# Thirty-five extra transposes of v in seven attention steps of a DMA-bound kernel

## The chip, the cores and the metric

The kernel runs on one core of one Trainium2 chip. The metric is the device time of one execution in microseconds, and a comparison is a difference of means over several executions.

In the lines of the profile PE is TensorE's matmuls and PEld its weight loads, DVE is VectorE, ACT is ScalarE, POOL is GpSimd and SP is SyncE; a q behind such a name is the engine's issuing of DMAs. A *fetch* is one DMA packet with a block of TensorE's own program (the row q8 instruction of a page: 41 packets, all of 16384 bytes, in the kernel before). A store has *landed* when all 16 of its completion packets have been written.

Three sources of numbers appear below, and they are kept apart. *Times* are of unprofiled executions and of the one profiled run. *Spans* are from the first to the last instruction in the profile; a span is usually about 1.7 us shorter than the time. *Trace positions* are times within the profiled run, counted from the start of its span.

## The reference, cut to what matters

Attention with a forgetting decay over 8 batches, 8 heads, 576 rows and head size 64; its result goes through a spectral mix with 64 modes, whose weights are two 64 x 512 x 512 float32 arrays.

```python
cum = np.cumsum(np.log(np.clip(f, 1e-4, 1.0)), axis=-1)
scores = scale * q @ k.T + cum[:, :, :, None] - cum[:, :, None, :]   # causal
attn = softmax(scores) @ v                     # (8, 8, 576, 64)
x = attn.transpose(0, 2, 1, 3).reshape(8, 576, 512)
X = rfft(x, axis=1)                            # modes 0..63 are mixed
Yr = Xr @ w_r - Xi @ w_i                       # per mode, 512 x 512
Yi = Xr @ w_i + Xi @ w_r
u = x + irfft(Y, n=576)
out = u + np.maximum(u @ w_ch, 0.0)            # (8, 576, 512) f32
```

The mode weights are 64 x 512 x 512 x 2 x 4 bytes = 134 MB as float32 in memory. They are streamed once through a ring of nine tiles, and they are what the kernel waits for: from 287.9 to 400.2 us their transfers make up 110.9 of the 112.3 us of the chain of waits in the trace of the kernel before.

## The kernel before

Attention runs in 32 steps, one head of a pair of batches at a time. Each step transposes five blocks of v back into rows. This is the place that the change touches:

```python
NRING = 9
STG = 3
...
def emit_vback(s):
    dc, bp, h = steps[s]
    c0 = 2 * bp * H + 2 * dc + h
    vp = psT.tile([128, NSB, 2, Dh], BF16, tag="tr", name="vp")
    for sc in range(NSB):                       # NSB = 5 blocks
        nc.tensor.transpose(
            vp[:, sc, :, :].rearrange("p b d -> p (b d)"),
            VTs[s // 2 % 2][:, h, sc * 128 : (sc + 1) * 128],
            ident_bf[:, :],
        )
    va = vap.tile([128, NSB, 2, Dh + 1], BF16, tag="va", name="va")
    nc.vector.tensor_copy(va[:, :, :, 0:Dh], vp[:, :, :, :])
    ...
```

The weights are loaded ahead into the ring and used tile by tile; a load is issued when its slot comes free:

```python
wpool = ctx.enter_context(tc.tile_pool(name="wpool", bufs=NRING))
...
def emit_w_load(n):                             # on GpSimd's DMA queue
    ...
    for t, src in enumerate((moe_w_r, moe_w_i)):
        pool_dma(wb[t:128:2, :, :], src[...])
...
def emit_modes(n, fill=None):                   # the matmuls on tile n, into A
    ...
    if n == NT - 1:                             # the last tile
        for mi in range(nm):
            ...                                 # matmuls on the weights
            fill(mi, hf)                        # matmuls of the first output job
            add_y(mi, mi + 1)
```

After the last tile come the output jobs. For each, TensorE makes `pu` and `pz` in PSUM, ScalarE copies `pu`, VectorE joins both, and SyncE issues the stores:

```python
def emit_u(job, ps, u, split=False):
    ...
    nc.scalar.copy(u[:, bs, :], ps[0][:, bs, :])

def emit_o(job, ps, u, o, pair, split=False):
    ...
    nc.vector.scalar_tensor_tensor(
        o[:, bs, :], ps[1][:, bs, :], 0.0, u[:, bs, :], ALU.max, ALU.add)
    ...
    nc.sync.dma_start(out[...], o[...])         # 27 stores in all
...
for n, job in enumerate(jobs):
    last = n == len(jobs) - 1
    zs = terms(job, ps, 1, "xy" if n else "y")
    ...
    run(zs, us)
    ...
    emit_u(jobs[n + 1], nxt, uo_n[0])
    emit_o(job, ps, *uo, n == 0)
```

The softmax here doesn't subtract the row's maximum and nothing guards it: scores larger than these inputs give would overflow.

## Time and profile before

The time was 436.51 us, the median of 3 runs (436.29 to 437.32).

| point in the trace of before | us |
|---|---|
| attention's last transposes of v begin | 268.9 |
| last weights landed | 400.2 |
| VectorE's last output instruction ends | 427.1 |
| span ends | 435.2 |

The rows of the page that matter, and the chain of waits, are shown in the prediction. (It counts the page's 40 slices from 0; this text counts them from 1.)

### The profile page before, as it was taken

To read this page: it belongs to the slowest core of one execution; us is meant where nothing else is said; L and a number is where in the kernel's file an instruction comes from. 1 tells how busy PE (TensorE), PEld (TensorE's weight loads), DVE (VectorE), ACT (ScalarE), POOL (GpSimd) and SP (SyncE) were. 2 spreads that over 40 slices of the span, in tenths; PEclk is the share of its full clock that TensorE was granted. 3 is DMA by queue.
4 is the path that set the end of the run, shared out by engine and by line. 5 is a ranking of instruction groups with operands and counts; after the bars stand their busy time and mean duration, and the time that the engine had idled before them with its cause. 6 is when DMAs were issued, how large, how long until landed. Compare 5 with 4: busy or idle time off the path is not lost.

```text
span 435.2 us, 12314 instructions
## 1 busy us (share of the span) xinstructions
PE 368.1 (85%) x5313; PEld 249.7 (57%) x5313; DVE 263.7 (61%) x659; ACT 224.4 (52%) x339; POOL 126.8 (29%) x198
## 2 busy tenths in 40 slices
PE   3787799999987879778787788799999998899881
PEld 2454566776666666566565666656665555454540
DVE  5797888876555655555557568533332665553892
ACT  2887488774526454365462646134434443631781
POOL 8333332333233233232333222223223223200400
PEclk9996899996558665586565869589999999989997
DMA  8999999999999999999999999999999999995797
GB/s 184 234 235 241 234 236 238 235 212 236 234 215 236 225 224 237 210 238 233 214 237 211 212 211 212 211 211 211 211 211 211 212 210 211 211 211 100 253 367 274
DMA packets 50982, 97.38 MB, mean 224 GB/s; under 512 B 3792, under 2 KB 12976, under 8 KB 50928
## 3 DMA queue, kind: packets, MB, share of 16 engines
q0 software_dynamic: 46560, 86.09, 100.9%
q1 hardware_dynamic: 4368, 10.51, 6.7%
q8 instruction: 41, 0.67, 0.6%
q14 instruction: 13, 0.11, 0.1%
HBM read 163.73 MB, written 9.44 MB: 398 GB/s over the span
## 4 chain that ended last, share of the span: by engine, by line
PE 35%; DMA 26%; ACT 12%; DVE 10%; issue 4%; SPq 0%; DVEq 0%; POOL 0%; ACTq 0%
DMA wb<-in_moe_w_i_dram 25%; ACT E L576 8%; PE pav L614 7%; PE ps L569 7%; PE A L188 6%; PE tp L307 5%; PE px L657 2%; PE vp L541 2%; DVE QTs L322 2%; ACT KT L320 2%; ACT VT L326 2%; DVE XT L671 1%; DVE os L1005 1%; DVE E L591 1%; PE px L682 1%
## 5 line engine op out<-in xcount | busy, mean ns | idle before, releaser
L576 ACT ACTIVATE E<-ps 128x1024 bf16<-128x1024 f32 (+1 forms) x128 | 101.5, 851 | 26.1 <-PE ps L569 15.4
L93 POOL DMA_DIRECT2D wb<-in_moe_w_r_dram x64 | 42.5, 664 | 128.9 <-PE A L188 25.1
L188 PE MATMUL A<-XT,wb 128*128 128x16 bf16 x1984 | 69.9, 181 | 8.2 <-DMA wb<-in_moe_w_i_dram 3.8
L188 PEld LDWEIGHTS <-wb 128*128 128x128 bf16 x1984 | 63.5, 100 | 22.8 <-issue 11.9
L569 PE MATMUL ps<-QTs,KT 64*128 64x64 bf16 (+4 forms) x384 | 60.2, 334 | 16.6 <-ACT E L576 14.7
L93 POOL DMA_DIRECT2D wb<-in_moe_w_i_dram x64 | 42.3, 661 | 77.5 <-DMA wb<-in_moe_w_i_dram 32.5
L614 PE MATMUL pav<-va,E 128*128 128x65 bf16 (+1 forms) x1088 | 57.1, 214 | 3.2 <-DVE x_all L636 2.6
L614 PEld LDWEIGHTS <-E 128*128 128x128 bf16 (+1 forms) x1088 | 47.0, 118 | 16.9 <-issue 7.0
L591 DVE TENSOR_TENSOR E<-E,trimask 128x256 bf16<-128x256 bf16 (+2 forms) x128 | 36.9, 303 | 20.0 <-ACT E L576 19.8
L326 ACT COPY VT<-tp 128x640 bf16<-128x640 bf16 (+1 forms) x32 | 23.2, 761 | 33.4 <-PE tp L307 33.4
L867 ACT CAST XW<-pxw 128x512 bf16<-128x512 f32 x36 | 20.7, 586 | 35.9 <-PE pxw L860 28.3
L569 PEld LDWEIGHTS <-KT 64*128 64x128 bf16 x384 | 19.4, 100 | 33.6 <-issue 22.8
L860 PE MATMUL pxw<-wch,yy 128*128 128x512 bf16 x144 | 36.0, 388 | 0.0
L320 ACT COPY KT<-tp 128x640 bf16<-128x640 bf16 (+1 forms) x32 | 21.9, 749 | 26.0 <-PE tp L307 25.8
L910 ACT CAST XW<-pB 128x512 bf16<-128x512 f32 x36 | 21.0, 585 | 25.4 <-PE pB L828 25.3
L909 DVE CAST x_all<-pA 128x512 bf16<-128x512 f32 x36 | 24.9, 692 | 14.2 <-PE pA L828 12.5
L322 DVE COPY QTs<-tp 128x640 bf16<-128x640 bf16 (+1 forms) x32 | 23.4, 767 | 14.3 <-PE tp L307 14.0
L636 DVE TENSOR_TENSOR x_all<-pav,rcp 128x384 bf16<-128x384 f32 x64 | 29.1, 455 | 0.9
L625 DVE RECIPROCAL rcp<-pav 128x6 f32<-128x6 f32 x64 | 12.1, 189 | 25.1 <-PE pav L614 24.3
L828 PEld LDWEIGHTS <-ident_bf 64*64 64x64 bf16 (+1 forms) x348 | 15.7, 108 | 17.9 <-issue 9.3
L153 DVE TENSOR_TENSOR YTe<-A,Yacc 128x128 bf16<-128x128 f32 x16 | 5.9, 367 | 33.3 <-PE A L188 33.3
L541 PE MATMUL vp<-ident_bf,VT 128*128 128x128 bf16 x160 | 18.4, 261 | 4.6 <-DVE QTs L322 3.9
(142 smaller groups left out, 617.4 us busy)
## 6 DMA issues: line engine op xcount, KB each, us to landing
wb<-in_moe_w_r_dram POOLq DMA_DIRECT2D x62, 512.0 KB, 16.7
wb<-in_moe_w_i_dram POOLq DMA_DIRECT2D x62, 512.0 KB, 17.3
stv<-in_v_dram POOLq DMA_DIRECT2D x10, 576.0 KB, 15.2
out_dram<-os SPq DMA_DIRECT2D x10, 512.0 KB, 4.5
stk<-in_k_dram POOLq DMA_DIRECT2D x11, 288.0 KB, 15.3
stq<-in_q_dram POOLq DMA_DIRECT2D x11, 288.0 KB, 15.1
wx<-in_v_dram POOLq DMA_DIRECT2D x5, 576.0 KB, 15.4
out_dram<-uo SPq DMA_DIRECT2D x3, 512.0 KB, 3.6
```

What stands on the lines that cost most here:

```text
L93: keep(nc.gpsimd.dma_start(dst, src))
L188: ins = nc.tensor.matmul(A[:, eb, mi, :], lhsT=w_of(mi, eb * 128), rhs=x_of(m), start=(i == 0), stop=(i == len(terms) - 1),)
L320: nc.scalar.copy(rows(KTs[pr % 2][:, :, 0:S]), tv)
L322: ins = nc.vector.tensor_copy(rows(QT[pr][:, :, :]), tv)
L326: nc.scalar.copy(rows(VTs[pr % 2][:, :, 0:S]), tv)
L541: nc.tensor.transpose(vp[:, sc, :, :].rearrange("p b d -> p (b d)"), VTs[s // 2 % 2][:, h, sc * 128 : (sc + 1) * 128], ident_bf[:, :],)
L569: nc.tensor.matmul(ps[:, b, o : o + n], lhsT=KTs[pr % 2][bs, h, jb * 128 : (jb + 1) * 128], rhs=QT[pr][bs, h, jb * 128 + c0 : jb * 128 + c ...
L576: nc.scalar.activation(E[:, :, piece * 512 : piece * 512 + w], ps[:, :, 0:w], ACT.Exp, scale=scale,)
L591: nc.vector.tensor_tensor(dg, dg, tr, ALU.mult)
L614: nc.tensor.matmul(pav[64 * half : 64 * half + w, slot, :], lhsT=E[:, b, c : c + (w - 1) * st + 1 : st], rhs=va[:, jb, b, :], start=(n == ...
L636: nc.vector.tensor_tensor(xo, pi, ri, ALU.mult)
L860: nc.tensor.matmul(pxw[:, :], lhsT=xT[:, eb, i * 128 : (i + 1) * 128], rhs=wch[:, eb, :], start=(eb == 0), stop=(eb == NDC - 1),)
```

## The change

The change puts 35 more TensorE transposes into steps 16 to 22, five per step. They rewrite block 0 of v at the same place in PSUM with the same values, so nothing is computed differently. The intent is not the work but its 70 TensorE instructions (a weight load and a matmul each): TensorE's program is fetched in blocks of 16384 bytes (in the kernel before one fetch for every 254 recorded instructions in the mean), and 70 instructions more ahead of the tail let the block borders, and so the fetches, fall at other places among the last tiles and stores.

```diff
     NRING = 9
     STG = 3
+    VREP = range(16, 23)
...
-            for sc in range(NSB):
+            for sc in [0] * (5 if s in VREP else 0) + list(range(NSB)):
                 nc.tensor.transpose(
                     vp[:, sc, :, :].rearrange("p b d -> p (b d)"),
```

## The prediction

> **What bounds the kernel now.** I read the page's head and DMA rows first, then the chain of waits from 394 us to the end, then busy times by stage, then the DMA view of short windows, because the change claims to act on when instruction fetches happen.
>
> The page of the kernel before:
>
> ```profile
> span 435.2 us, 12314 instructions
> DMA  8999999999999999999999999999999999995797
> GB/s 184 234 235 241 234 236 238 235 212 236 234 215 236 225 224 237 210 238 233 214 237 211 212 211 212 211 211 211 211 211 211 212 210 211 211 211 100 253 367 274
> q8 instruction: 41, 0.67, 0.6%
> ```
>
> The 16 DMA engines are busy from the first slice to about 396 us: the weights stream at 211 to 240 GB/s without a hole. There is one hole of about 10 us (slice 36, 100 GB/s), and then the output stores. The q8 row is the fetch of TensorE's own program: 0.67 MB in 41 packets is 16384 bytes each, and the packet records of the trace confirm that size for all 41.
>
> The chain that ended last, from 394 us on, and the last issues:
>
> ```profile
> 384.77 15.42 DMA wb<-in_moe_w_i_dram
> 400.23 0.36 PE A L172 x8
> 401.31 0.86 PE plw L813 x4
> ...
> 421.62 1.24 DVE os L1005
> ...
> 425.46 0.63 PE pz L828 x4
> ```
>
> ```profile
> 426.46 0.68 DVE L1005 SCALAR_TENSOR_TENSOR uo<-pz,uo 128x512 f32<-128x512 f32 x1
> 428.25 2.49 SPq L1012 DMA_DIRECT2D out_dram<-uo  x2
> ```
>
> So there are three stages that set the end: the weights' last landing at 400.2 us; a tail of TensorE, ACT and DVE that makes output tiles (DVE ends at 427.1 us); and the stores, which end 6 us after DVE. In the packet records the last store's packets are written at 433.06 us. From 417 us on, the store queue is never empty, and each 512 KB store lands 1.22 to 1.26 us after the one before it (422.79, 424.01, 425.26, 426.49 us): the stores' end is bound by DMA bandwidth, and by the slowest of the 16 engines, because a store has landed only when all of them have.
>
> Busy times by stage (columns: stretch, its length, then busy time and count of PE, PEld, DVE, ACT, POOL, granted clock, DMA share, GB/s):
>
> ```profile
> 141.00:160.00 19.00, 15.89 (x240) 11.77 (x238) 11.31 (x31) 9.17 (x14) 5.84 (x9) 0.68 1.13 226
> 160.00:180.00 20.00, 16.43 (x209) 12.02 (x206) 10.34 (x30) 10.11 (x14) 6.27 (x10) 0.50 1.13 225
> 180.00:205.00 25.00, 20.91 (x306) 15.64 (x306) 15.37 (x40) 11.94 (x16) 7.04 (x12) 0.67 1.13 227
> 287.00:322.00 35.00, 35.00 (x515) 22.44 (x514) 11.46 (x31) 14.05 (x25) 11.70 (x17) 1.00 1.12 211
> 355.00:370.00 15.00, 13.07 (x204) 7.79 (x204) 8.50 (x17) 6.34 (x11) 5.00 (x7) 1.00 1.12 211
> 370.00:385.00 15.00, 13.02 (x144) 6.88 (x140) 7.86 (x16) 8.16 (x15) 3.28 (x6) 0.89 1.12 211
> ```
>
> In the steps that change (143 to 204 us) TensorE is busy 83% at a clock of 0.5 to 0.7. From 287 to 355 us it is busy all the time and works off a backlog. From 355 us on it idles again, because it waits for weights.
>
> [...]fetches come every 8 to 12 us, on average every 254 recorded TensorE instructions. [...] The packet records give the hold: 0.88 to 1.02 us beside weights, but 1.27 us at 405.21 us and 1.46 us at 416.25 us, among stores:
>
> ```profile
> q1 hardware_dynamic: 207, 0.77, 97.4%
> q8 instruction: 1, 0.02, 4.5%
> ```
>
> (the DMA view of 416 to 418 us.) [...] The trace shows 0.5 and 1.0 in turn up to 285 us, then 1.0.
>
> **The change part by part.** Nothing is removed. Each of steps 16 to 22 transposes block 0 of v six times instead of once, into the same PSUM place; the result is the same.
>
> First, TensorE work. 35 transposes are 35 weight loads and 35 matmuls, 70 instructions. The five transposes of a step start 94 to 100 ns apart in steps 16, 18, 19, 20, 21, 22 and 55 ns apart in step 17 (full clock). Sum: 5 x (95 + 55 + 96 + 100 + 94 + 100 + 94) ns = 3.2 us. The built programs show that the scheduler also moves some neighbours in those steps, and that the last 5,717 of TensorE's instructions are the same in both; GpSimd's and SyncE's order does not change.
>
> Second, whether that reaches the weights. The queue of weights is deep: a 512 KB transfer lands 13 to 20 us after its issue, though one takes 2.4 us at 211 GB/s. The shallowest place is the issue at 279.80 us, which lands at 292.6 us; the transfer ahead of it ends at 288.3 us. Issued 3.2 us later, at 283.0 us, it still has 5 us of queue ahead. So the DMA has no hole and the last weights land at 400.2 us as before.
>
> Third, whether TensorE is in time for them. From each tile's landing and its first matmul, TensorE's lag is 34.5 us at 277 us, 7.9 us at 322 us, 0.9 us at 355 us, and from then on it is 0.7 us or less: it waits for weights. It idles 41.0 - 36.3 = 4.7 us between 355 and 396 us. A backlog larger by at most 3.2 us is gone before the last tile. Cost on the path: 0.
>
> Fourth, the fetches. In the tail each block border comes 70 instructions sooner. Counting back 70 TensorE instructions from where they are now: 396.93 goes to about 395.5 us, 405.21 to about 401.1 us, 416.25 to about 413.6 us. And a border that lay just past the end (10433 + 254 = 10687 of 10665 recorded) now lies inside: old place 10617, about 423.4 us. So 42 fetches instead of 41, if a fetch is made that near the end.
>
> What each is worth: 396.93 to 395.5 stays on an engine that is busy with weights, same hold: 0. 405.21 to 401.1 moves from the first stores into the hole, where DMA does nothing; but the store queue runs dry once more at 412 us, so what it cost was already given back: 0 to -0.2. 416.25 to 413.6: now it hits the first packets of a new batch. The completion packets of the store issued at 415.17 us are written by 15 engines at 417.3 to 417.4 us and by the last about 1.9 us later; the lag of this one engine is 1.0 us at 422 us and about 0.45 us at 428 us [...], and at the end the last engine ends at 433.06 us where most end by 432.4 us. Moved to 413.6 us, it has the dips at 415.7 and 419.4 us to catch up: worth up to -0.7 us. The new fetch at 423.4 us has only the dip at 425.6 us, worth about 0.5 us by the same engine's record: it starts 1.3 to 1.5 us late and ends 0.8 to 1.0 us late, so +0.8 to +1.0. Sum: about +0.1 to +0.3 us if the 42nd fetch is made (I give this 0.75), about -0.7 us if not. Expected: about 0; I add 0.1 us for the risk of the backlog: 436.6 us.
>
> **The rivals.** (a) The added transposes reach the end: the backlog of TensorE is not worked off, since some idle time after 355 us belongs to waits on ACT and DVE rather than on weights. Against it: 4.7 us of idle time for 3.2 us. It would give 437.5 to 439. (b) The fetches cost more than their ring time: a fetch on the engine that carries the last weights (396.93 us now) sets the landing at 400.2 us, or the one at 405.21 us holds up the moves of yl that the first output tiles need. Then the move to 401.1 us, or a changed overlap, gains about 1 us: 435.3 to 435.8. For it: at 405 us moves that landed 1.7 us after issue begin to take 3.2 us. Against it: the tiles that need those moves come some 6 us later. (c) The clock: [...] It would show as a higher granted clock from 143 to 205 us, and still give nothing, since the DMA queue sets the weights' end.
>
> **Range and chances.** Everything that can move is of the size of one fetch, 0.5 to 1.5 us, on 436.5 us; three runs of the kernel before spread over 1.0 us. So 435.6 to 437.7 us should hold it 8 times in 10. 2% is 8.7 us; nothing here comes near: faster 0.01, within 2% 0.98, slower 0.01.
>
> **What would show each step.** Transposes: vp has 195 matmuls instead of 160, DMA keeps 211 GB/s to 396 us, and the chain's last weights land within 0.5 us of 400.2 us. Backlog: TensorE's idle time from 355 to 396 us falls from 4.7 to 1.5 to 3 us. Fetches: q8 counts 42; in the tail they stand near 395.5, 401, 413.6 and 423.4 us. End: the completion packets of the stores after 424 us have one straggler, and between 416 and 422 us hardly any. I am wrong if the last weights land later than 401 us, if the count stays 41 and the time falls by 0.6 us or more, or if the stores' end moves by more than 1 us with DVE's end in place.

The sum came to "about +0.1 to +0.3 us" if the 42nd fetch is made, and its terms (0 to -0.2, up to -0.7, +0.8 to +1.0) are estimates from the trace of the kernel before. The "0.5 and 1.0 in turn" are the granted TensorE clock. The hole and the dips that it names are these in the same trace: the DMA share was 0.00 and 0.02 in the two microseconds from 401 to 403 us, 0.78 from 412 to 413 us, 0.86 from 415 to 416 us, 0.76 from 419 to 420 us and 0.90 from 425 to 426 us, and 0.94 to 1.08 in the other microseconds from 408 to 431 us.

## More of the kernel before

One more row is needed later, the granted TensorE clock in tenths:

```profile
PEclk9996899996558665586565869589999999989997
```

Each of its 40 digits is about 10.9 us of the span. From the tenth slice to the twenty-seventh (about 98 to 294 us) the clock is mostly below full and often near half; after that it is nearly always full.

## The result, and the profile after

The changed kernel took 437.19 us, the median of 6 runs (436.66 to 437.87), against 436.40 us (436.16 to 437.32) for 6 runs of the kernel before in the same rounds. The ratio is 1.0017, with a 95% interval of 1.0004 to 1.003: the mean time of one kernel's runs over that of the other's of the same rounds, so not quite the ratio of the two medians. It is within 2%, and about 0.7 us slower. All outputs are right. The profiled run of the changed kernel was its fastest (436.66 us), so its span of 434.9 us must not be read as a gain over 435.2 us.

First the page of the changed kernel:

```profile
span 434.9 us, 12366 instructions
PEclk9996899998767957759557778699999999999997
GB/s 188 232 235 241 234 236 239 235 212 236 233 216 236 224 225 237 212 237 232 216 237 212 211 212 211 211 211 212 211 211 211 211 211 211 211 211 105 245 389 260
q8 instruction: 42, 0.69, 0.6%
```

The GB/s row is the old one to within a few digits: the weights stream as before. There is one fetch more. The clock row is higher than before in many of the slices from the tenth on. That begins ahead of the change, whose first step lies at 143 us in the fourteenth slice, and so it must not be put down to the change without more.

The instructions on the tile vp, kernel before and then kernel after (count, then minimum, median and maximum in ns, first and last start):

```profile
L541 PE MATMUL vp<-ident_bf,VT x160: 216/230/315, 22.4 to 268.9; 128*128 128x128 bf16 x160
```

```profile
L542 PE MATMUL vp<-ident_bf,VT x195: 216/222/314, 22.4 to 264.7; 128*128 128x128 bf16 x195
```

The 35 transposes are there, and the last transpose of the kernel starts 4.2 us *earlier*, not later. Busy times by stage show how (kernel after; the columns are those in the prediction):

```profile
141.00:160.00 19.00, 15.80 (x257) 12.14 (x254) 11.89 (x32) 9.19 (x14) 5.96 (x9) 0.77 1.13 226
160.00:180.00 20.00, 16.41 (x243) 12.79 (x238) 10.77 (x32) 10.26 (x14) 6.52 (x10) 0.69 1.13 225
180.00:205.00 25.00, 19.34 (x350) 14.95 (x348) 14.88 (x44) 14.53 (x19) 6.85 (x12) 0.80 1.13 227
```

The granted clock rose from 0.68, 0.50 and 0.67 to 0.77, 0.69 and 0.80. TensorE does more matmuls in less busy time. Is it the change that does this? In one pair of traces it looks so, but the 14 traces of the whole study are more careful witnesses:

| | granted clock, 98 to 141 us | granted clock, 143 to 204 us | attention's last transpose of v begins, us | TensorE idle, 355 to 396 us |
|---|---|---|---|---|
| repeats in steps 16 to 22 (after, `a2`, `s256`, `s256b`) | 0.73, 0.78, 0.75, 0.73 | 0.75, 0.75, 0.75, 0.70 | 263.8 to 265.8 | 5.1 to 6.5 |
| no repeats there (10 traces, the kernel before among them) | 0.62 to 0.82, mean 0.69 | 0.61 to 0.72, mean 0.66 | 263.3 to 269.5 | 3.3 to 6.7 |

From 143 us on the clock is higher with the repeats, though the best of the ten others (0.72) passes the lowest of the four. But the same four traces had a clock above the others' mean already from 98 to 141 us, before any repeat. So it is not shown that the repeats raise the clock. When attention ends, and how long TensorE idles later, overlaps fully. Two traces of one and the same program (`end36` and `end36b`, below) begin that last transpose at 269.5 and at 264.0 us, so the 4.2 us between before and after are within what unchanged code does. Neither moved the end, because the weights set it: the last of them landed at 399.33 to 400.67 us in all 14 traces. The idle time of TensorE ahead of the last weights, in the kernel before and then after, is what is left of these stretches:

```profile
355.00:396.00 41.00, 36.33 (x514) 20.96 (x512) 22.22 (x41) 19.12 (x33) 8.58 (x13) 0.96 1.09 205
```

```profile
355.00:396.00 41.00, 34.66 (x494) 20.01 (x495) 22.02 (x41) 18.57 (x32) 8.60 (x13) 1.00 1.09 206
```

41.00 - 36.33 = 4.7 us became 41.00 - 34.66 = 6.3 us. The chain that ended last, kernel after, from its last weights on (start in us, us, what):

```profile
384.31 15.42 DMA wb<-in_moe_w_i_dram
399.74 0.05 issue
399.78 0.36 PE A L173 x8
...
423.75 1.22 DVE os L1006
...
425.01 0.63 PE pz L829 x4
```

The last weights landed at 399.74 us instead of 400.2 us, and all that follows in TensorE and VectorE keeps that distance (VectorE's last output instruction ends at 426.69 us instead of 427.14 us). What differs is the DMA engines' work. The DMA view of 416 to 418 us, where the kernel before had a fetch (shown in the prediction), has in the kernel after only stores (packets, MB, and the time of the packets as a share of 16 engines):

```profile
q1 hardware_dynamic: 227, 0.81, 101.8%
```

and the DMA view of 425 to 427 us, kernel before and then after:

```profile
q1 hardware_dynamic: 271, 0.65, 96.1%
```

```profile
q1 hardware_dynamic: 269, 0.75, 97.6%
q8 instruction: 1, 0.02, 2.9%
```

The fetch of 416.25 us has moved ahead of those stores, and a new one stands among the final ones. In the packet records the fetches from 396 us on are these, with the time that each held its engine:

| | before | predicted after | after |
|---|---|---|---|
| among the last weights | 396.93 (0.88 us) | 395.5 | 396.73 (0.88 us) |
| before or in the first stores | 405.21 (1.27 us) | 401.1 | 401.61 (1.35 us) |
| in the later stores | 416.25 (1.46 us) | 413.6 | 413.96 (0.94 us) |
| new, the 42nd | none | 423.4 | 425.48 (0.92 us) |

### A ruler for the tail

Single runs of either kernel spread over about 1 us or more, so one needs a measure with less noise. From the end of the last matmul on weights (called *the last A*) to VectorE's end is 26.45 to 26.68 us in all 14 traces, whether before, after or an experiment. What comes before the last A is the arrival of weights and the clock, and it moved by 1.4 us between traces (399.98 to 401.38 us). What comes after VectorE's end is stores and fetches. So I compare the time from the last A to the landing of the last store, and call it *the tail*.

The numbers in the next table come from the records of the stores' landings and of the fetch packets. All times are counted from the last A; stores are numbered 0 to 26.

| | tail | fetches, at | store 10 | store 11 | store 17 | store 20 | store 26, the last |
|---|---|---|---|---|---|---|---|
| before | 32.79 | 4.6, 15.7 | 15.8 | 19.1 | 24.7 | 26.6 | 32.8 |
| after | 32.99 | 1.5, 13.8, 25.3 | 17.5 | 18.7 | 24.3 | 27.5 | 33.0 |

Before, the fetch at 15.7 us shows as a jump of 3.3 us between stores 10 and 11. After, that fetch comes earlier (13.8 us), and store 17 is 0.4 us ahead. Then the new fetch shows as a jump of 1.6 us between stores 19 (25.9) and 20 (27.5), and the lead is lost. How far the last of a store's 16 completion packets is behind the median one tells the same: before, 1.97 us at store 11 and still 0.69 us at store 26, 13.7 us later; after, 1.67 us at store 20 and still 1.22 us at store 26, 5.5 us later. So 1.28 us were made up behind the one fetch, and 0.45 us behind the later one. There is one pair of traces here; the experiments give more. (The kept traces do not say on which of the 16 DMA engines a packet ran; that one engine lags is read from the times of a store's 16 completion packets.)

### The profile page after: what moved, and what is told of

It is laid out like the page before. It is cut to its first block, busy times and chain, and to the rows that moved or that the text cites. A ratio compares the mean times of both kernels' runs of the same rounds, so it can differ in the third digit from the quotient of the medians.

```text
span 434.9 us, 12366 instructions
## 1 busy us (share of the span) xinstructions
PE 359.5 (83%) x5330; PEld 248.3 (57%) x5348; DVE 263.9 (61%) x659; ACT 224.7 (52%) x339; POOL 127.7 (29%) x198
## 4 chain that ended last, share of the span: by engine, by line
DMA 40%; PE 26%; ACT 9%; DVE 7%; issue 4%; SPq 0%; DVEq 0%; POOL 0%; ACTq 0%
DMA wb<-in_moe_w_i_dram 39%; ACT E L577 6%; PE pav L615 6%; PE A L189 5%; PE ps L570 5%; PE tp L308 4%; PE vp L542 2%; DVE QTs L323 2%; ACT KT L321 2%; PE pz L829 1%; DVE os L1006 1%; PE px L658 1%; ACT VT L327 1%; DVE x_all L637 1%; PE px L683 1%
## 5 line engine op out<-in xcount | busy, mean ns | idle before, releaser
L189 PE MATMUL A<-XT,wb 128*128 128x16 bf16 x1984 | 71.9, 181 | 14.1 <-DMA wb<-in_moe_w_i_dram 9.0
L570 PE MATMUL ps<-QTs,KT 64*128 64x64 bf16 (+4 forms) x384 | 55.7, 318 | 14.4 <-ACT E L577 12.3
L615 PE MATMUL pav<-va,E 128*128 128x65 bf16 (+1 forms) x1088 | 54.5, 207 | 6.8 <-DVE x_all L637 6.1
L615 PEld LDWEIGHTS <-E 128*128 128x128 bf16 (+1 forms) x1088 | 44.6, 113 | 17.1 <-DVE x_all L637 8.1
L861 PE MATMUL pxw<-wch,yy 128*128 128x512 bf16 x133 | 32.9, 379 | 1.2 <-issue 0.7
L323 DVE COPY QTs<-tp 128x640 bf16<-128x640 bf16 (+1 forms) x32 | 23.4, 768 | 14.1 <-PE tp L308 13.8
L542 PE MATMUL vp<-ident_bf,VT 128*128 128x128 bf16 x195 | 20.5, 255 | 4.5 <-DVE QTs L323 3.8
## 6 DMA issues: line engine op xcount, KB each, us to landing
wb<-in_moe_w_i_dram POOLq DMA_DIRECT2D x62, 512.0 KB, 17.5
```

Source lines behind the costliest of these rows:

```text
L189: ins = nc.tensor.matmul(A[:, eb, mi, :], lhsT=w_of(mi, eb * 128), rhs=x_of(m), start=(i == 0), stop=(i == len(terms) - 1),)
L323: ins = nc.vector.tensor_copy(rows(QT[pr][:, :, :]), tv)
L542: nc.tensor.transpose(vp[:, sc, :, :].rearrange("p b d -> p (b d)"), VTs[s // 2 % 2][:, h, sc * 128 : (sc + 1) * 128], ident_bf[:, :],)
L570: nc.tensor.matmul(ps[:, b, o : o + n], lhsT=KTs[pr % 2][bs, h, jb * 128 : (jb + 1) * 128], rhs=QT[pr][bs, h, jb * 128 + c0 : jb * 128 + c ...
L615: nc.tensor.matmul(pav[64 * half : 64 * half + w, slot, :], lhsT=E[:, b, c : c + (w - 1) * st + 1 : st], rhs=va[:, jb, b, :], start=(n == ...
L861: nc.tensor.matmul(pxw[:, :], lhsT=xT[:, eb, i * 128 : (i + 1) * 128], rhs=wch[:, eb, :], start=(eb == 0), stop=(eb == NDC - 1),)
```

## The experiments

These are the theories, as the expectations letter them. **F1**: the 42nd fetch, among the final stores, costs the time. **F2**: the changed places of the fetches that were there before matter too, as gain or loss. (**F** is both.) **W**: the transposes' work in steps 16 to 22 (or what it does to the clock) reaches the end. And all of it may be noise, since 0.7 us is 0.16%.

All means below are of one kernel's runs of one call, 6 of the kernel tried and 11 of the kernel before. The three calls had the means 436.93, 437.04 and 436.91 us for the kernel before.

### The changed kernel again, and the kernel before as its own control

Two runs without any edit: `a2` is the changed kernel, `b2` the kernel before.

> The changed kernel again, unchanged: a second trace and a tighter interval. If the difference is real, 436.9 to 437.4 us against 436.3 to 436.6 of the kernel before, ratio 1.001 to 1.003. Its trace should again have 42 fetches on queue 8, the last at about 425.5 us after the span's start, and one DMA engine whose packets of the last stores end 0.8 to 1.2 us after most others'; if the straggler at the end is missing and the time is as high, the fetch theory is in trouble.

> The kernel before against itself: the control. Every theory says ratio 1 within its interval (about plus or minus 0.0015). Its trace is a second look at the tail of the kernel before: from the last matmul on weights to the last store's landing 32.80 us in the first trace; theory F1 expects 32.2 to 32.9 us here, where the runs with a fetch among the last stores have 32.9 to 34.9 us.

`a2` took 437.65 us in the median (437.01 to 438.02), 0.70 us more in the mean than the kernel before, ratio 1.0017 (1.0002 to 1.0032). The first result repeats, with 42 fetches, the last at 426.31 us; the last of the 16 completion packets of the last store was 1.24 us behind the median one. `b2` took 436.35 us (436.08 to 436.95), 0.51 us *less* than the same code in the same rounds, ratio 0.9989 (0.9975 to 1.0004). So one comparison of 6 with 11 runs is uncertain by some 0.5 us, and every single difference below is to be read with that. The DMA view of 425 to 427 us of `b2` has no fetch, as in the first trace of the kernel before:

```profile
q1 hardware_dynamic: 233, 0.60, 89.2%
```

### The same 70 instructions, elsewhere

Theory W stands or falls with where the work is. `early` moves it to steps 0 to 6:

```diff
-    VREP = range(16, 23)
+    VREP = range(0, 7)
```

> The same 35 repeated transposes in steps 0 to 6 instead of 16 to 22: TensorE's tail is shifted by the same 70 instructions, and steps 16 to 22 are as before. Theory F (the places of the fetches in the tail, the 42nd among them): as the changed kernel, +0.4 to +1.0 us on the kernel before, ratio 1.001 to 1.0025. Theory W (the work itself: attention steps 16 to 22, the clock and the arrival of the last weights): as before, within 0.2 us, ratio 0.9995 to 1.0005.

`early` took 437.28 us (436.81 to 438.65), +0.47 us in the mean, 1.0011 (0.9995 to 1.0027).

`st35` is the kernel before, with 35 tiny transposes at the very start, where TensorE has nothing to do (its first matmul in the kernel before starts 6.13 us into the span); they are thrown away:

```diff
+        for n_wm in (18, 17):
+            wm = psT.tile([128, NSB, 2, Dh], BF16, tag="tr", name="wm")
+            for _ in range(n_wm):
+                keep(
+                    nc.tensor.transpose(
+                        wm[0:8, 0, 0, 0:8], ident_bf[0:8, 0:8], ident_bf[0:8, 0:8]
+                    )
+                )
```

> The same with 35 tiny transposes: 70 instructions, the changed kernel's shift without its work; ten instructions more than the run before this one. The last fetch should appear at about 425.5 us. Theory F1: +0.4 to +1.0 us on the kernel before and +0.5 to +1.2 us on the run with 30. Theory F2: as the run with 30 within 0.2 us. Theory W (work in steps 16 to 22): both within 0.2 us of the kernel before.

`st35` took 437.16 us (436.63 to 438.47), +0.32 us, 1.0011 (0.9993 to 1.0029). Its DMA view of 425 to 427 us shows the fetch among the final stores:

```profile
q1 hardware_dynamic: 264, 0.73, 97.7%
q8 instruction: 1, 0.02, 3.0%
```

Each of the two is inside the noise alone; their 12 runs together have the mean 437.38 us. But their fetches, counted from the last A, are at 1.3, 13.3 and 25.0 us in `early`, and at 1.7, 13.6 and 25.4 us in `st35`, as in the changed kernel (1.5, 13.8, 25.3), and so are their tails: 32.98 and 33.06 us beside 32.99 and, in `a2`, 32.89 us. Work in steps 16 to 22 isn't needed for what the changed kernel does to the tail.

### A whole block: the work stays, the borders go back

If it is the borders, then as many instructions more as lie between two of them must look like none. In the trace of the kernel before a fetch comes every 254 recorded instructions in the mean; 256 were added. `s256` is the changed kernel with 93 tiny transposes at the start (the block above, with `(47, 46)`), 70 + 186 = 256 instructions more than before. `s256b` is a second run of it. `st128` is the kernel before with `(64, 64)`: 256 instructions, and no repeats of v.

> The changed kernel with 93 tiny transposes more at the very start, where TensorE has nothing to do: 256 more instructions than before in all, so that one whole block more is fetched and the tail's block borders fall on the same instructions as in the kernel before. Theory F: the time of the kernel before within 0.2 us, ratio 0.9995 to 1.0005, fetches near 396.9, 405 and 416 us and none at 425 us. Theory W: +0.4 to +1.0 us, as the changed kernel.

> The changed kernel with 93 tiny transposes at the start once more, unchanged: it had the time of the kernel before less 0.4 us, with an interval that holds 1. Theory F: ratio 0.998 to 1.0003, and 0.6 us or more below the changed kernel's +0.7 us. If it comes out above 1.001, the first result was noise and theory W (the work in steps 16 to 22) is open again.

> 128 tiny transposes at the start and no repeated v: 256 instructions, the tail's borders as in the kernel before, one block more fetched in all. Theory F1: no fetch among the last stores and the kernel before's time within 0.3 us, ratio 0.9993 to 1.0007. If the run with 93 of them and the repeated v was really faster than the kernel before, and the tiny transposes at the start are why, it is 0.3 to 0.7 us faster here as well.

The first `s256` took 436.46 us (435.91 to 437.13), -0.44 us, 0.999 (0.9976 to 1.0004), 1.1 us less in the mean than `a2` in the same rounds. The repeat took 437.20 us with a spread of 3.6 us (435.81 to 439.37), +0.55 us, 1.0014 (0.9987 to 1.004). The repeat contradicts the first in time; by the expectation for it, that would reopen theory W. Both together (12 runs, mean about 436.97 us) decide nothing. `st128` took 436.25 us (435.76 to 437.16), -0.63 us, 0.9987 (0.9971 to 1.0003), which is 0.1 us from its control `b2`.

The traces are clearer than the times. The pages of `s256b` and `st128` have 42 fetches, one more than that of the kernel before, but the DMA view of 425 to 427 us has none in either run of `s256`, nor in `st128`. Here are `s256b` and then `st128`:

```profile
q1 hardware_dynamic: 291, 0.79, 103.6%
```

```profile
q1 hardware_dynamic: 260, 0.63, 96.9%
```

The tails are 32.23, 32.56 and 32.86 us, those of the kernel before (32.79, and 32.45 in `b2`). What made the profiled run of `s256` slow (437.13 us, its slowest) lies ahead of the last A: TensorE ended the last tile 1.5 us after its weights' landing (401.38 against 399.91 us), where the kernel before took 0.40 us (the eight matmuls in its chain). The granted clock had fallen to half from 365.1 to 368.5 us and again from 385.5 to 389.0 us. Three of the 14 traces have a dip at 385 to 389 us (`s256`, `st128`, `end36b`), and these end the last tile 1.5, 1.4 and 1.0 us after its landing; the other eleven, with earlier dips or none, take 0.40 to 0.41 us. So a late dip of the clock goes with a late last A, though no run was made to test it. This is one source of the scatter, with the landing of the last weights (399.33 to 400.67 us over the traces) as the other.

### The 42nd fetch alone

`end36` is the kernel before, with 36 tiny matmuls after the last useful one. Their results go nowhere. All earlier instructions, and so all earlier block borders, stay where they were; only the end of the program moves past the next border.

```diff
+    NEND = 36
...
+        pe_end = psPair[0]["u"].tile([128, 2, D], F32, tag="u", name="pend")
+        for _ in range(NEND):
+            keep(add(pe_end[0:8, 0, 0:8], ident_bf[0:64, 0:8], ident_bf[0:64, 0:8], True))
```

> The kernel before with 36 tiny matmuls (8 columns, result unread) after TensorE's last useful matmul, at about 426 us: the fetches at 397, 405 and 416 us stay, and only the last fetch is added, at about 426 to 428 us among the last stores. Theory F1 (the 42nd fetch alone costs): +0.5 to +1.0 us. Theory F2 (the other fetches' new places cost): within 0.2 us of the kernel before. Theory W: within 0.2 us too.

> The kernel with 36 tiny matmuls at the end once more, unchanged, for a tighter interval on the added last fetch alone. Theory F1: ratio 1.0005 to 1.002 again, so that both together exclude 1. Theory F2: ratio within 0.0005 of 1.

`end36` took 437.03 us (436.65 to 438.36), +0.41 us, 1.001 (0.9994 to 1.0025). Repeated as `end36b` it took 437.85 us (437.54 to 439.3), +1.02 us, 1.0024 (1.0008 to 1.004). Together, 12 runs have the mean 437.70 us.

The DMA view of 425 to 427 us of `end36`:

```profile
q1 hardware_dynamic: 266, 0.64, 92.3%
q8 instruction: 1, 0.02, 3.3%
```

The fetch is at 26.2 us from the last A (the next store to land, number 21, comes 2.4 us after number 20 instead of 1.2 us), the old two are still at 4.4 and 15.6 us, store 17 lands at 24.8 us as in the kernel before (24.7), and the tail is 33.55 us. In `end36b` store 17 is at 24.8 us again. Then comes a fetch that held its engine for 1.80 us:

```profile
q1 hardware_dynamic: 268, 0.98, 97.2%
q8 instruction: 1, 0.02, 4.5%
```

(427 to 429.5 us), store 21 lands 3.9 us after store 20 instead of 1.2 us, and the tail is 34.86 us. The end of the two timelines, the kernel after first and then `end36b` (SPq is SyncE's issue of stores):

```profile
426.01 0.68 DVE L1006 SCALAR_TENSOR_TENSOR uo<-pz,uo 128x512 f32<-128x512 f32 x1
427.68 2.46 SPq L1013 DMA_DIRECT2D out_dram<-uo  x2
```

```profile
426.69 0.68 DVE L1006 SCALAR_TENSOR_TENSOR uo<-pz,uo 128x512 f32<-128x512 f32 x1
430.06 1.41 SPq L1013 DMA_DIRECT2D out_dram<-uo  x2
```

The last two issues start 1.0 and 2.1 us after VectorE's end in the changed kernel, and 2.7 and 3.2 us after it in `end36b`. The 36 matmuls, which took about 1 us from 426.2 us on in `end36b`, lie off the path: no other instruction waits for them. So a fetch among the final stores, with no other change but these, makes the stores end later. (A control with so few matmuls that the border is not reached was not run.)

### Two borders at the end

`end164` has `NEND = 164`, to put two borders past the last useful matmul.

> The kernel before with 164 tiny matmuls after TensorE's last useful one: 328 instructions more, two fetches more, both among the last stores (about 426 and 429 us). Theory F1: at least as slow as with one added fetch, +0.6 to +1.4 us on the kernel before, ratio 1.0013 to 1.003, since a later fetch leaves its DMA engine less time to catch up. Theory F2 and W: within 0.2 us of the kernel before.

It took 439.17 us (437.86 to 440.02), +1.99 us, 1.0046 (1.0029 to 1.0063). But only one of its two late fetches stands among the stores (428.24 us; tail 33.54 us, as `end36`). The other came at 438.36 us, after the span's last instruction. The time exceeds the span by 1.9 to 3.4 us here, where 1.7 to 1.8 us is usual; so about 1.0 us of the 2.0 us lies outside the span (2.73 us in the mean, against 1.73). It does not say what a second fetch among the stores would cost, which was its purpose.

### Smaller shifts

`st30` and `st20` are the kernel before with the start block of `(15, 15)` and `(10, 10)` transposes: shifts of 60 and of 40 instructions.

> The kernel before with 30 tiny transposes (8 by 8) at the very start and nothing else: the tail shifted by 60 instructions. Fetches expected at about 397, 402 and 414.5 us, and none among the last stores, since the block border now falls behind TensorE's last matmul. Theory F1 (only the added last fetch costs): 0 to -0.4 us on the kernel before, ratio 0.999 to 1.0003. Theory F2 (the new places of the other fetches cost): +0.4 to +1.0 us, as the changed kernel, ratio 1.001 to 1.0025.

> 20 tiny transposes at the start: a shift of 40 instructions, small enough, I estimate, that the last block border stays behind TensorE's last instructions (at 60 it was still before them). Theory F1: no fetch at 425 to 428 us, and 0 to -0.5 us on the kernel before (the fetch at 405 us moves to about 404 us, the one at 416 us to about 415 us). Theory F2 (any new place of those two costs): +0.3 us or more. If a fetch still stands at 426 us, F1 says +0.2 to +0.8 us instead, and the run tells nothing of F2.

I had expected that 60 instructions leave the last border outside the program. That was wrong: `st30` has a fetch at 426.25 us. It took 437.05 us (436.68 to 438.22), +0.24 us, 1.0006 (0.9991 to 1.0022). Its trace is worth more than its time: the fetch before the last came at 14.5 us from the last A instead of 13.3 to 13.8 us, store 17 landed at 25.0 us, no sooner than in the kernel before, and the tail is 33.62 us. Its fetch at 1.6 us is where `st35` has it (1.7), so that one alone brings no gain; the gain up to store 17 goes with the other fetch, and 10 instructions less and it is not there. This is one trace, of the slowest of its six runs (438.22 us).

`st20` has no fetch among the final stores; its last one came at 436.04 us, after the last store had landed. Yet it took 437.31 us (436.73 to 437.49), +0.32 us, 1.0009 (0.9993 to 1.0025), and its one tail is 33.46 us. F1 does not explain that. Its fetches at 2.8 and 16.0 us are in no other kernel at just these places, and store 17 is 0.5 us late (25.2 us) already, so F2 might; one trace does not settle it. About 0.1 us of the 0.32 us lies outside the span, as in `end164`: the time exceeds the span by 1.86 us in the mean.

### All together

Times, pooled by what they do to the borders:

| group | kernels | runs | mean, us | standard error |
|---|---|---|---|---|
| kernel before | all calls, and `b2` | 45 | 436.82 | 0.09 |
| same borders as before, more instructions | `s256`, `s256b`, `st128` | 18 | 436.74 | 0.24 |
| borders 70 sooner, with a 42nd fetch | after, `a2`, `early`, `st35` | 24 | 437.41 | 0.11 |
| old borders, and a 42nd fetch | `end36`, `end36b` | 12 | 437.70 | 0.21 |

Tails, one trace for each kernel:

| group | tail | store 17 from the last A | from store 17 to the last landing |
|---|---|---|---|
| borders as before (before, `b2`, `s256`, `s256b`, `st128`) | 32.58 (32.23 to 32.86) | 24.77 | 7.81 |
| 70 sooner (after, `a2`, `early`, `st35`) | 32.98 (32.89 to 33.06) | 23.99 | 8.99 |
| `end36`, `end36b` | 33.55, 34.86 | 24.8, 24.8 | 8.8, 10.1 |

The first two groups of tails just fail to overlap (32.86 and 32.89 us). The difference of 0.40 us is a gain of 24.77 - 23.99 = 0.78 us up to store 17 and a loss of 8.99 - 7.81 = 1.18 us after it.

Over all 14 traces, with `st30`, `st20` and `end164` too, these two parts sort cleaner than the tails. The eight traces with a fetch among the final stores (25.0 to 27.5 us) take 8.44 to 10.08 us from store 17 to the last landing, and the six without take 7.51 to 8.22 us. The four traces whose fetch in the later stores (third row of the table of fetches above) is at 13.3 to 13.8 us have store 17 at 23.70 to 24.32 us, and the ten others, with it at 14.5 us or later, at 24.57 to 25.24 us.

The times have 437.41 - 436.82 = 0.59 us; the 0.2 us between that and 0.40 us is no larger than the errors. The pooled groups were not all run in the same rounds, so the table supports the single comparisons and does not replace them.

Not every expected size came true. `early` (+0.47 us) is where F1 had put it. `end36` (+0.41) and `st35` (+0.32) came out just below what F1 said, `end36b` (ratio 1.0024) just above. `st128` (-0.63 us) and the first `s256` (-0.44 us) are faster than F allows, as the control `b2` is (-0.51 us). `st35` is not 0.5 us above `st30` (+0.09 us in the mean), since `st30` has the late fetch too.

No kernel beats the kernel before by more than its own control does: `st128` with 436.25 us stands beside `b2` with 436.35 us (medians). A program with the early place of the one fetch and without the late one would be the candidate. It was not built: in the tails of the 14 traces the second and third of these fetches are 269 to 312 recorded instructions apart, and a shift at the start moves them all.

## Why the prediction was right or wrong

The time came out at 437.19 us, inside the range and 0.6 us above the value of 436.6 us. The range of 435.6 to 437.7 us would have held no effect at all just as well, so that the number fell into it says little for the mechanism. By its own steps:

- **What is added.** 195 transposes instead of 160: right. Their cost on the path was 0, as said.
- **The weights' end.** Right: 211 GB/s to the end, last landing 399.74 us, within 0.5 us of 400.2.
- **The backlog.** The step "TensorE's idle time from 355 to 396 us falls from 4.7 to 1.5 to 3 us" failed; it rose to 6.3 us. The backlog did not grow by 3.2 us: tile 32 of the weights was first used at 273.1 us instead of 277.5 us. Rival (c), that the added work raises the clock, may have a part in this, but it is not shown. The granted clock from 143 to 204 us was 0.70 to 0.75 in the four traces with the repeats, against 0.66 in the mean without. But these four had 0.73 to 0.78 from 98 to 141 us, before the repeats, against a mean of 0.69. Scatter between traces, with which I had not reckoned, is enough for all of it: the idle time that I read as 4.7 us lies between 3.3 and 6.7 us in traces without the repeats, so a fall of 2 to 3 us could not have been read from one trace in any case. As rival (c) itself said, nothing of this reaches the end, for the weights set it.
- **The fetches' places.** Three came within 0.4 to 1.2 us of where counting back 70 instructions put them (counted from the last A, unchanged code moves them by up to 1.1 us: 15.7 us before, 16.8 us in `b2`). The 42nd, given 0.75, was made, but at 425.5 us and not at 423.4 us. The step at fault is the spacing: I used the program's mean of 254 recorded instructions from fetch to fetch, and in the tail it is 270 (before, 498 left to 228 left) to 286 (after, 560 left to 274 left). 274 - 286 is below 0, so the fetch stands when no recorded TensorE instruction is left. There are fewer stores behind it in which its engine could catch up: six, over which the last completion packet came nearer to the median one by 0.45 us (1.67 to 1.22 us).
- **The sum.** The mechanism, a gain from the moved fetch and a loss from the new one, is what the tails show. Their sum was put at +0.1 to +0.3 and measured +0.40 in the tails, +0.59 in the pooled times. Which of the two terms was mis-sized stays open. Split at store 17, the moved fetch, "up to -0.7", gave -0.78, and the new one, "+0.8 to +1.0", cost +1.18. By the times the new fetch alone (`end36`, `end36b`) cost 437.70 - 436.82 = 0.88 us, as predicted, and then the moves gave back only 437.70 - 437.41 = 0.29 us. No run has the moved fetch without the new one.
- **The straggler.** "Between 416 and 422 us hardly any" was wrong. In the stores of about 420 to 425 us (numbers 14 to 16) the last completion packet was still 0.22 to 0.95 us behind the median one in the four kernels with the borders 70 sooner, against 0.79 to 1.49 us in the five with the old borders: less, but there. At the last store it was 0.88 to 1.24 us behind in the four, and 0.29 to 0.69 us in the five: that half was right.
- **Rivals.** (a) fell: nothing of the transposes reached the end. (b) is not tested by itself for the fetch at 401.6 us; the last weights did not come late with it, and in `st30` that fetch's move alone brought no gain.
- **Readings that were off.** Fetches do not all come 8 to 12 us apart: in the trace of the kernel before the gaps go from 6.1 to 18.6 us. The clock was not full all the time from 285 us on: it was at half from 381.0 to 384.4 us. The weights that were issued at 279.80 us landed at 290.8 us by the landing record, not at 292.6 us, and over the whole run a transfer of weights lands 9.5 to 20.6 us after its issue. None of this changes a step, since the transfer ahead of that one does end at 288.3 us. And the terms of the sum as written (0 to -0.2, -0.7, +0.8 to +1.0) add up to -0.1 to +0.3 us, not to +0.1 to +0.3.

What stays open: why `st20` is not faster than it was, how the sum divides between the two fetches, and what remains of 0.2 us between tails and times.

## What to carry to other kernels

When a kernel ends in a DMA-bound run of stores, ask what else uses the DMA engines there; in this case fetches of TensorE's own program did. In the traces of before and after each held its DMA engine for 0.88 to 1.03 us while the weights streamed and for 0.92 to 1.46 us after that, and in `end36b` the one among the final stores for 1.80 us. Here one fetch more cost about 0.9 us in the last 10 us (`end36` and `end36b`), where little behind it gave the time back (0.45 of 1.67 us in the kernel after). Do not trust a difference of 0.1% from one comparison: run the same code against itself, and find a stretch of the trace (here from the last matmul on weights to the last landing) in which the noise of the rest is absent. And before a difference between two traces is put down to a change, look at how far traces of the same code differ in the same number: here the end of attention moved by 5.5 us between two traces of one program.
